# Transposing f and x from rows of four tokens, with the sigmoid and the drive term walking by row position

## The chip, the cores and the metric

The kernel runs on one core of a Trainium2 chip. The metric is the time on the device in microseconds, the median of several runs. A run of this kernel can fall into a slower state: the unchanged kernel gave 400.4 to 402 us in most of its runs and 409 to 437 us in some, on several chips. A ratio of two kernels is the mean time of one's fast runs over the mean time of the other's fast runs of the same rounds, so it is not quite the ratio of the medians that are quoted.

Names: PE is the tensor engine, PEld its weight loads, ACT the scalar engine, DVE the vector engine, POOL GpSimd, which issues the fetches of f and x, SP the engine that issues the transposing DMAs and the output stores. In a chain of waits, a q behind a name is that engine's sequencer, and "issue" is time for which the profile shows no wait.

## The reference, cut to what matters

```python
# x, f_logit: (4, 6144, 256); lower_bound: (256,)
sig = 1.0 / (1.0 + np.exp(-f_logit))
f = lower_bound + (1.0 - lower_bound) * sig
for t in range(S):                       # a recurrence over the tokens
    h = f[:, t] * h + (1.0 - f[:, t]) * x[:, t]
    y[:, t] = h
# then, for all 24576 tokens:
g = np.maximum(y @ w1, y @ w2)           # 256 -> 1024
out = g @ w_out                          # 1024 -> 256
```

## The kernel before

The work goes in 48 blocks of 512 tokens. Feature numbers lie on partitions, tokens along the free dimension. So f and x have to be transposed: the first blocks by the tensor engine, the other 44 (chunks of 1,024 tokens) by transposing DMAs from a bf16 scratch copy in DRAM. Per block there are four dependent steps: the sigmoid `u` on ACT, the decay `ff = 1 + nom*u` on DVE, the drive term `v = u*x` on DVE, and the scan over the tokens on DVE, which gives `y`. PE then multiplies: `dT` is the first layer, evicted by ACT as `rt`; `psO` is the second layer, evicted by DVE as `osb`. (max(a, b) = a + relu(b - a), so `dT` holds y(w2 - w1), ACT takes the relu, and y times w1 w_out goes straight into `psO`; the factor 1 - lower_bound of y lies in these weights.)

```python
def cross(c):                                   # one chunk: two transposing DMAs
    nt = chunks[c][2]
    for s in range(2):
        if by_xbar(c, s):
            dst = inpool.tile([P, KC, CH], BF16, name=("fT", "xT")[s])
            nc.sync.dma_start_transpose(
                out=dst[:, :, 0:nt], in_=held[c, s][0:nt, :])
            held[c, s] = dst
# ...
def gate(j):                                    # the sigmoid
    # ...
    nc.scalar.activation(
        out=like(u[:, :, 0:nb], fT), in_=fT, func=AF.Sigmoid, scale=-1.0)
# ... in scan_steps(j): decay(0), decay(1), drive, scan(0), scan(1)
def drive():
    xT = turned[j, 1]
    nc.vector.tensor_tensor(
        out=like(v[:, :, 0:nb], xT), in0=like(u[:, :, 0:nb], xT), in1=xT, op=ALU.mult)
# ... the steady loop; a turn works on block j's matmuls and prepares block j + 1
    gates = {}
    if j + 1 < NBLK and by_xbar(blocks[j + 1][3], 0):
        gates[0] = j + 1
    if j + 2 < NBLK and not by_xbar(blocks[j + 2][3], 0):
        gates[FC // 2] = j + 2
    # ...
    for fc in range(FC):
        first_layer(j, fc)                      # two matmuls to dT, ACT evicts to rt
        second_layer(j - 1, fc)                 # five matmuls to psO
        # ...
        if fc in gates:
            gate(gates[fc])
        if fc == 0 and 2 < j < NBLK - 1:
            scans = scan_steps(j + 1)
        if fc < len(scans):
            scans[fc]()
```

The sigmoid of block j + 1 is issued on ACT behind the first eviction of block j. And `dT` has three PSUM buffers.

## Time and profile before

| | before |
|---|---|
| time, median of 3 | 400.79 us (400.66 to 400.88) |
| the profiled run | 430.05 us, a slow one; span 428.3 us |
| PE, ACT, DVE busy | 392.8, 268.5, 248.7 us |
| u, v, one instruction | 1,054 and 688 ns |
| undisturbed period of a block | 7.82 us |

From the page of the kernel before: the busy times, the counts of DMA packets, the queue that holds the transposes and output stores, and the shares of the chain of waits that ended last.

```profile
PE 392.8 (92%) x2744; PEld 296.8 (69%) x2792; DVE 248.7 (58%) x359; ACT 268.5 (63%) x447; POOL 26.4 (6%) x58
...
DMA packets 103377, 77.01 MB, mean 180 GB/s; under 512 B 93552, under 2 KB 94064, under 8 KB 102640
...
q1 hardware_dynamic: 100512, 51.13, 66.7%
...
PE 46%; DMA 34%; SPq 15%; ACT 3%; DVE 1%; issue 1%; ACTq 0%
```

The chain gives 34% to DMAs, but this run is a slow one, 29 us longer than the timed ones. Durations of single instructions can be taken from it (`u` and `v` take 1,051 and 684 ns in the fast run e1, too); its waits belong to the slow state. The fast profile nearest to this kernel is that of run e1 below (wide rows, but the old compute); its chain is nearly all PE, and there too a block takes 7.82 us (`u` starts at 329.67 and 337.49):

```profile
PE 94%; DMA 2%; DVE 2%; issue 1%; SPq 1%; DVEq 0%
```

The groups of instructions of the kernel before; the columns are busy us and mean ns of one, then the engine's idle time before them and what ended most of it.

```profile
L389 ACT ACTIVATE rt<-dT 128x512 bf16<-128x512 f32 x384 | 219.2, 598 | 104.1 <-PE dT L381 100.0
L381 PE MATMUL dT<-y,wd 128*128 128x512 bf16 x720 | 219.5, 384 | 21.3 <-ACT rt L389 19.5
...
L190 ACT ACTIVATE u<-fT 128x1024 bf16<-128x1024 bf16 x44 | 46.4, 1054 | 35.5 <-DMA fT<-scr_1_91 18.2
L220 DVE TENSOR_TENSOR v<-u,xT 128x1024 bf16<-128x1024 bf16 x44 | 30.3, 688 | 3.8 <-DMA xT<-scr_0_92 1.8
```

One undisturbed block on DVE, from the timeline of the kernel before (start, duration):

```profile
375.32 0.62 DVE L209 TENSOR_SCALAR ff<-u,nom 128x512 bf16<-128x512 bf16 x2 [1.38 <-ACT u L190]
375.85 0.68 DVE L220 TENSOR_TENSOR v<-u,xT 128x1024 bf16<-128x1024 bf16 x1
377.16 0.69 DVE L430 COPY osb<-psO 128x512 f32<-128x512 f32 x1 [0.63 <-PE psO L410]
377.77 2.45 DVE L233 TENSOR_TENSOR_SCAN y<-ff,y,v 128x512 bf16<-128x512 bf16 x2
```

DVE has gaps of 1.38 and 0.63 us here: the recurrence has room inside PE's period.

### The profile page before, as it was taken

The page shows a single profiled execution, that of the slowest core. Times are in us where ns is not written, and L with a number is a line of the kernel's source. Part 1 is how long each engine was busy: PE and PEld are TensorE (multiplying, and loading weights), DVE is VectorE, ACT ScalarE, POOL GpSimd, SP SyncE. Part 2 cuts the span into 40 slices and gives each one's busy share as a digit, 9 for nine tenths or more (in the row PEclk, how much of TensorE's full clock was granted, in tenths as well). Part 3 has the DMA queues.
Part 4 walks back from the last instruction along what each step waited for, and adds up shares of the span by engine and source line. Part 5 has one row for each costly group of instructions (what it writes and reads, how often), then busy time and mean ns, then how long its engine had stood idle before and what let it go on. Part 6 is the DMA issues. An engine that isn't in the chain of part 4 may idle for free.

```text
span 428.3 us, 6970 instructions
## 1 busy us (share of the span) xinstructions
PE 392.8 (92%) x2744; PEld 296.8 (69%) x2792; DVE 248.7 (58%) x359; ACT 268.5 (63%) x447; POOL 26.4 (6%) x58
## 2 busy tenths in 40 slices
PE   3999979798789999998997899999998999999996
PEld 1677756576557777776775577767676777777775
DVE  5785637455357566564653557657547656567551
ACT  3656656557366676675673666756657676776762
POOL 1400000000000000000000000000000000000000
PEclk9999999999989999999999699999999999999999
DMA  7999999999999999999998999999999999998112
GB/s 245 222 220 198 123 157 141 137 169 252 81 240 226 119 239 233 112 248 168 183 237 75 218 158 186 250 145 170 219 131 231 226 216 164 268 157 179 79 69 100
DMA packets 103377, 77.01 MB, mean 180 GB/s; under 512 B 93552, under 2 KB 94064, under 8 KB 102640
## 3 DMA queue, kind: packets, MB, share of 16 engines
q1 hardware_dynamic: 100512, 51.13, 66.7%
q0 software_dynamic: 2544, 25.17, 36.1%
q8 instruction: 22, 0.36, 0.4%
q10 hardware_dynamic: 288, 0.26, 0.2%
q14 instruction: 11, 0.09, 0.1%
HBM read 53.48 MB, written 48.23 MB: 237 GB/s over the span
## 4 chain that ended last, share of the span: by engine, by line
PE 46%; DMA 34%; SPq 15%; ACT 3%; DVE 1%; issue 1%; ACTq 0%
PE psO L410 25%; DMA fT<-scr_0_90 20%; PE dT L381 19%; SPq L153 13%; DMA fT<-scr_1_91 12%; ACT u L190 2%; DMA w1n_110<-in_moe_w_dram 2%; SPq L433 1%; PE psO L352 1%; ACT rt L389 1%; PE tT L180 1%; PE psO L365 0%; SPq L121 0%; DVE osb L430 0%; DVE y L233 0%
## 5 line engine op out<-in xcount | busy, mean ns | idle before, releaser
L389 ACT ACTIVATE rt<-dT 128x512 bf16<-128x512 f32 x384 | 219.2, 598 | 104.1 <-PE dT L381 100.0
L381 PE MATMUL dT<-y,wd 128*128 128x512 bf16 x720 | 219.5, 384 | 21.3 <-ACT rt L389 19.5
L410 PE MATMUL psO<-wob,rt 128*128 128x256 bf16 x1536 | 230.7, 274 | 2.7 <-issue 0.4
L410 PEld LDWEIGHTS <-rt 128*128 128x128 bf16 x1536 | 170.7, 114 | 41.4 <-issue 1.1
L233 DVE TENSOR_TENSOR_SCAN y<-ff,y,v 128x512 bf16<-128x512 bf16 x88 | 107.9, 1268 | 0.1
L430 DVE COPY osb<-psO 128x512 f32<-128x512 f32 x94 | 64.7, 690 | 59.0 <-PE psO L410 58.9
L381 PEld LDWEIGHTS <-wd 128*128 128x128 bf16 x768 | 75.8, 99 | 33.2 <-issue 24.6
L209 DVE TENSOR_SCALAR ff<-u,nom 128x512 bf16<-128x512 bf16 x94 | 29.0, 351 | 105.0 <-ACT u L190 105.0
L410 PE MATMUL psO<-w_109,y 128*128 128x256 bf16 x384 | 74.0, 275 | 0.0
L410 PEld LDWEIGHTS <-y 128*128 128x128 bf16 x384 | 43.4, 113 | 42.6 <-issue 3.5
L190 ACT ACTIVATE u<-fT 128x1024 bf16<-128x1024 bf16 x44 | 46.4, 1054 | 35.5 <-DMA fT<-scr_1_91 18.2
L220 DVE TENSOR_TENSOR v<-u,xT 128x1024 bf16<-128x1024 bf16 x44 | 30.3, 688 | 3.8 <-DMA xT<-scr_0_92 1.8
L98 POOL DMA_DIRECT2D scr_0_90<-in_f_logit_dram x11 | 5.4, 493 | 149.7 <-DMA fT<-scr_0_90 149.7
L98 POOL DMA_DIRECT2D scr_1_91<-in_f_logit_dram x11 | 5.3, 486 | 148.8 <-DMA fT<-scr_1_91 148.1
L233 DVE TENSOR_TENSOR_SCAN y<-ff,v 128x512 bf16<-128x512 bf16 x6 | 7.0, 1208 | 0.0
L98 POOL DMA_DIRECT2D scr_0_92<-in_x_dram x11 | 5.4, 488 | 18.7 <-DMA xT<-scr_0_92 16.9
L98 POOL DMA_DIRECT2D scr_1_93<-in_x_dram x11 | 5.3, 486 | 15.7 <-DMA xT<-scr_1_93 14.9
L190 ACT ACTIVATE u<-tT 128x1024 bf16<-128x1024 bf16 x3 | 3.2, 1058 | 4.3 <-PE tT L180 4.3
L352 PE MATMUL psO<-ident_f,w1n_110 128*128 128x128 f32 x8 | 1.9, 422 | 3.4 <-DMA w1n_110<-in_moe_w_dram 3.4
L341 ACT ACTIVATE wd<-wdf,om 128x128 bf16<-128x128 f32 (+1 forms) x6 | 2.2, 428 | 4.3 <-DVE wdf L333 4.3
L352 PEld LDWEIGHTS psO<-ident_f,w1n_110 128*128 128x128 f32 x8 | 1.6, 221 | 3.7 <-issue 3.7
L220 DVE TENSOR_TENSOR v<-u,tT 128x1024 bf16<-128x1024 bf16 x3 | 3.6, 1216 | 0.0
(49 smaller groups left out, 45.1 us busy)
## 6 DMA issues: line engine op xcount, KB each, us to landing
out_dram<-osb SPq DMA_DIRECT2D x47, 512.0 KB, 4.8
scr_0_90<-in_f_logit_dram POOLq DMA_DIRECT2D x11, 512.0 KB, 7.5
scr_0_92<-in_x_dram POOLq DMA_DIRECT2D x11, 512.0 KB, 12.4
scr_1_91<-in_f_logit_dram POOLq DMA_DIRECT2D x11, 512.0 KB, 7.9
scr_1_93<-in_x_dram POOLq DMA_DIRECT2D x11, 512.0 KB, 13.6
fn<-in_f_logit_dram POOLq DMA_DIRECT2D x3, 256.0 KB, 7.9
xn<-in_x_dram POOLq DMA_DIRECT2D x3, 256.0 KB, 8.6
w2n_112<-in_moe_w_dram SPq DMA_DIRECT2D x1, 512.0 KB, 6.5
```

What stands on the lines that cost most here:

```text
L98: nc.gpsimd.dma_start(out=scr[0:nt, :].rearrange("(p i) d -> p (i d)", p=P), in_=src.rearrange("(p i) d -> p (i d)", p=P),)
L153: nc.sync.dma_start_transpose(out=dst[:, :, 0:nt], in_=held[c, s][0:nt, :])
L180: nc.tensor.transpose(dst, src, ident[:])
L190: nc.scalar.activation(out=like(u[:, :, 0:nb], fT), in_=fT, func=AF.Sigmoid, scale=-1.0)
L209: nc.vector.tensor_scalar(out=ff[:, h, 0:nb], in0=u[:, h, 0:nb], scalar1=nom[:, h : h + 1], scalar2=1.0, op0=ALU.mult, op1=ALU.add,)
L220: nc.vector.tensor_tensor(out=like(v[:, :, 0:nb], xT), in0=like(u[:, :, 0:nb], xT), in1=xT, op=ALU.mult,)
L233: nc.vector.tensor_tensor_scan(out=y[:, h, 0:nb], data0=ff[:, h, 0:nb], data1=v[:, h, 0:nb], initial=init, op0=ALU.mult, op1=ALU.add,)
L352: nc.tensor.transpose(pt[:, kc, q, :], half(w1n, g)[:, kc, 2 * r + q], ident_f[:])
L381: nc.tensor.matmul(dT[:, 0:nb], lhsT=wd[:, kc, fc * P : (fc + 1) * P], rhs=y[:, kc, 0:nb], start=(kc == 0), stop=(kc == KC - 1),)
L389: nc.scalar.activation(out=rt[:, 0:nb], in_=dT[:, 0:nb], func=AF.Relu)
L410: nc.tensor.matmul(ps[:, r, :], lhsT=left, rhs=right, start=(s == 0 and (r == 0 or j == NBLK - 1)), stop=(s == n - 1 and (r == 1 or j == N ...
L430: nc.vector.tensor_copy(out=osb[:, 2 * g : 2 * g + 2, :], in_=ps[:])
```

## The change

The intent is to make the source rows of the transposing DMA longer. A row of 512 B holds one token; the change reads rows of 2 KB, four tokens. The transpose then delivers tokens 0, 4, 8, ... together, then 1, 5, 9, ..., and so on. The sigmoid and the drive term therefore walk by row position: they read `fT` and `xT` contiguously, and write `u` (and read `u` and write `v`) at a stride of 4 elements, 8 B, so that `u` and `v` come out in token order.

```diff
+    RT = 4
+    wide_rows = (True, True)
@@ cross(c)
-                dst = inpool.tile([P, KC, CH], BF16, name=("fT", "xT")[s])
-                nc.sync.dma_start_transpose(
-                    out=dst[:, :, 0:nt], in_=held[c, s][0:nt, :]
-                )
-                held[c, s] = dst
+                dst = inpool.tile([P, RT, KC, CH // RT], BF16, name=("fT", "xT")[s])
+                nc.sync.dma_start_transpose(
+                    out=dst[:].rearrange("p i k r -> p (i k) r"),
+                    in_=held[c, s][0:nt, :].rearrange("(r i) d -> r (i d)", i=RT),
+                )
+                held[c, s] = dst[:].rearrange("p i k r -> p k r i")
@@ gate(j)
+        out = like(u[:, :, 0:nb], fT)
+        if by_xbar(blocks[j][3], 0):
+            out, fT = by_row(out), by_row(fT)
+        nc.scalar.activation(out=out, in_=fT, func=AF.Sigmoid, scale=-1.0)
+    def by_row(t):
+        return t if len(t.shape) == 3 else t.rearrange("p k m i -> p k i m")
@@ drive()
+            operands = [like(v[:, :, 0:nb], xT), like(u[:, :, 0:nb], xT), xT]
+            if by_xbar(c, 1):
+                operands = [by_row(t) for t in operands]
  ... (cut: like() takes m from its source; slices by o // RT; the old forms under else)
```

More of the change, by code (lines that the diff above doesn't have):

```diff
@@ L151, in cross @@
             if by_xbar(c, s):
-                dst = inpool.tile([P, KC, CH], BF16, name=("fT", "xT")[s])
-                nc.sync.dma_start_transpose(
-                    out=dst[:, :, 0:nt], in_=held[c, s][0:nt, :]
-                )
-                held[c, s] = dst
+                if wide_rows[s]:
+                    dst = inpool.tile([P, RT, KC, CH // RT], BF16, name=("fT", "xT")[s])
[4 more added lines that the diff above has]
+                    held[c, s] = dst[:].rearrange("p i k r -> p k r i")
+                else:
+                    dst = inpool.tile([P, KC, CH], BF16, name=("fT", "xT")[s])
+                    nc.sync.dma_start_transpose(
+                        out=dst[:, :, 0:nt], in_=held[c, s][0:nt, :]
+                    )
+                    held[c, s] = dst
     def turn_steps(j):
@@ L162, in turn_steps @@
             if by_xbar(c, s):
-                turned[j, s] = held[c, s][:, :, o : o + nb]
+                if wide_rows[s]:
+                    turned[j, s] = held[c, s][:, :, o // RT : (o + nb) // RT, :]
+                else:
+                    turned[j, s] = held[c, s][:, :, o : o + nb]
                 continue
@@ L189, in gate @@
         fT = turned[j, 0]
-        nc.scalar.activation(
-            out=like(u[:, :, 0:nb], fT), in_=fT, func=AF.Sigmoid, scale=-1.0
-        )
+        out = like(u[:, :, 0:nb], fT)
+        if by_xbar(blocks[j][3], 0):
+            out, fT = by_row(out), by_row(fT)
+        nc.scalar.activation(out=out, in_=fT, func=AF.Sigmoid, scale=-1.0)
         us[j] = u
@@ L197, in like @@
             return t
-        return t.rearrange("p k (m i) -> p k m i", m=P)
+        return t.rearrange("p k (m i) -> p k m i", m=src.shape[2])
+    def by_row(t):
+        return t if len(t.shape) == 3 else t.rearrange("p k m i -> p k i m")
     def scan_steps(j):
@@ L219, in drive @@
             xT = turned[j, 1]
+            operands = [like(v[:, :, 0:nb], xT), like(u[:, :, 0:nb], xT), xT]
+            if by_xbar(c, 1):
+                operands = [by_row(t) for t in operands]
             nc.vector.tensor_tensor(
-                out=like(v[:, :, 0:nb], xT),
-                in0=like(u[:, :, 0:nb], xT),
-                in1=xT,
-                op=ALU.mult,
+                out=operands[0], in0=operands[1], in1=operands[2], op=ALU.mult
             )
```

## The prediction

> **What bounds the kernel now.** The tensor engine, in the timed runs. The profiled run (430.05 us against 400.79 timed) is no fair picture of them.
>
> - In undisturbed stretches (timeline, from 347 us on) a block of 512 tokens repeats every 7.82 us: 16 matmuls of 512 columns and 40 of 256.
> - The steady loop starts at 40.0 us. Without stalls, its 45 periods would have to start at 419.97 - 45 x 7.82 = 68.1 us. So some 28 us of the profile are stalls of PE.
> - The chain of waits charges them to the transposing DMAs: 20% + 12% on fT. They land 16.1 and 15.5 us after issue (xT: 9.4 and 9.1); ACT waits 35.5 us for fT, PE 19.5 us for ACT's evictions.
> - 428.3 - 28 = 400.3 us of span, plus the 1.75 us by which this run's time exceeds its span, is 402. The timed runs took 400.79: they have practically none of these stalls. I blame the recording of 103,377 DMA packets.
>
> **What the change moves.** No instruction is added or reordered.
>
> 1. The 44 transposes move the same 512 KB, from 256 rows of 2 KB in place of 1,024 of 512 B. 93,552 packets are under 512 B, about 2,048 per transpose: 256 B each. If wide rows let a packet carry more, that count and the landing times fall.[...] I expect 256 B packets to stay, since contiguous 512 B rows are read so now. Then landing changes little, or worsens with the stride.
> 2. The drive term v (44 x 688 ns) loses step 1 on u and v.[...] The slow v from PSUM takes 1,216 ns, so I expect 1.22 us: +0.53 us per block, +23 us of DVE in all (248.7 to about 272).
> 3. The sigmoid u (1,051 ns) writes at a stride; I expect 1.05-1.15 us.
>
> **How much is critical.** Of (1), nothing in timed runs. Of (2): in the loop, v ends 0.63 us before the psO is ready that the copy after it needs, and the scans end at 380.22 us, 0.65 us before PE needs y at 380.87. The +0.53 us is absorbed before the copy; 0.1 and then 0.65 us are left.
>
> **Prediction.** 400.8 us: the same. Range 399.7 to 404.0. Faster by over 2%: 0.02 (PE has no 8 us to give). Within 2%: 0.90. Slower by over 2%: 0.08.
>
> **What the profile would show.** v<-u,xT at 1.2 us; u<-fT at 1.05; the same 7.82 us period; packets under 512 B near 93,500 if rows don't matter, far fewer if they do. The profiled span may move (405 to 440) alone.
>
> **What would make this wrong.** [...]v over 1.95 us, or u and v together over 1.28 us longer, puts the recurrence on PE's path; each further 0.1 us costs about 4.4 us over 44 blocks. Reads of 256 B at a 2 KB stride so slow that transposes miss their two-block lead: the timed runs would stall as the profile does. Or timed runs that do hide several us of DMA stalls, which shorter landings would save.

`v` at 1.22 us, an estimate from the 1,216 ns of `v` from PSUM in the profile before, is +0.53 us per block, `u` at 1.05 to 1.15 us is next to nothing, both are absorbed, and the sum is 400.8 us, the same.

## The result

| | before | after |
|---|---|---|
| time, median of 4 | 400.84 us (one of the 4 slow, 409.82) | 472.24 us (471.55 to 473.03) |
| ratio of fast runs | | 1.1784 (95%: 1.1754 to 1.1813), slower |
| u, v, one instruction | 1,054 and 688 ns | 2,512 and 2,471 ns |
| period of a block | 7.82 us | 9.44 us |

The profiled run of the changed kernel is a fast one, span 471.1 us. The same lines of its page:

```profile
PE 407.5 (87%) x2744; PEld 291.7 (62%) x2792; DVE 315.0 (67%) x359; ACT 321.3 (68%) x447; POOL 26.7 (6%) x58
...
DMA packets 103377, 77.01 MB, mean 163 GB/s; under 512 B 93552, under 2 KB 94064, under 8 KB 102640
...
q1 hardware_dynamic: 100512, 51.13, 43.8%
...
DVE 53%; ACT 25%; PE 11%; issue 7%; DMA 2%; SPq 1%; ACTq 0%
```

The number of packets is the same to the last one: with rows of 2 KB, too, the transposes go in packets of 256 B (both traces list 90,112 of exactly that size, 2,048 for each of the 44 transposes). DMAs have gone from the chain; ACT and DVE are in their place. The groups:

```profile
L406 ACT ACTIVATE rt<-dT 128x512 bf16<-128x512 f32 x384 | 216.9, 612 | 129.2 <-PE dT L398 128.3
L398 PE MATMUL dT<-y,wd 128*128 128x512 bf16 x720 | 224.7, 382 | 49.5 <-DVE y L250 44.4
...
L206 ACT ACTIVATE u<-fT 128x1024 bf16<-128x1024 bf16 x44 | 110.5, 2512 | 0.0
L240 DVE TENSOR_TENSOR v<-u,xT 128x1024 bf16<-128x1024 bf16 x44 | 108.7, 2471 | 0.0
```

`u` and `v` take 2.4 and 3.6 times as long, and PE waits 44.4 us for `y`. No engine is at its limit, though: ACT and DVE are busy 68% and 67%. The chain in order of time over one block shows why this still costs (start, duration, what):

```profile
399.32 2.53 ACT u L206
401.85 0.02 issue
401.87 0.04 DVE ff L226
401.91 0.23 issue
402.14 0.35 DVE ff L226
402.49 2.38 DVE v L240
404.87 0.52 DVE osb L447
405.39 2.37 DVE y L250 x2
407.76 0.04 issue
407.80 0.39 PE dT L398
408.19 0.02 issue
408.21 0.02 ACTq L406
408.23 0.04 issue
408.27 0.04 ACT rt L406
408.31 0.45 issue
408.77 2.50 ACT u L206
```

This is a loop through three engines: `u` of a block, its decay, its drive term, a copy that stands between, its two scans, its first matmul, the eviction of that, and only then the `u` of the next block, which is queued behind that eviction. This turn takes 408.77 - 399.32 = 9.45 us; over the whole chain, from the `u` that starts at 41.01 to the one at 446.55, 43 turns take 9.43 us each. 44 turns at 9.43 in place of 7.82 us are 71 us more, and the measured difference is 472.24 - 400.84 = 71.4 us. In that loop the slower `u` and `v` stand with +1.46 us (2,507 - 1,051 ns, the medians) and +1.78 us (2,470 - 687). Without them it would take about 6.2 us, so by this estimate the kernel before had about 1.6 us of its 7.82 per block to spare (the expectations below were written with 9.44 us and so with 1.62).

### The profile page after: what moved, and what is told of

It is laid out like the page before. It is cut to its first block, busy times and chain, and to the rows that moved or that the text cites. A ratio compares the mean times of both kernels' runs of the same rounds, so it can differ in the third digit from the quotient of the medians.

```text
span 471.1 us, 6970 instructions
## 1 busy us (share of the span) xinstructions
PE 407.5 (87%) x2744; PEld 291.7 (62%) x2792; DVE 315.0 (67%) x359; ACT 321.3 (68%) x447; POOL 26.7 (6%) x58
## 2 busy tenths in 40 slices
DMA packets 103377, 77.01 MB, mean 163 GB/s; under 512 B 93552, under 2 KB 94064, under 8 KB 102640
## 3 DMA queue, kind: packets, MB, share of 16 engines
q1 hardware_dynamic: 100512, 51.13, 43.8%
q0 software_dynamic: 2544, 25.17, 32.8%
## 4 chain that ended last, share of the span: by engine, by line
DVE 53%; ACT 25%; PE 11%; issue 7%; DMA 2%; SPq 1%; ACTq 0%
ACT u L206 24%; DVE v L240 22%; DVE y L250 22%; PE dT L398 6%; DVE osb L447 5%; PE psO L427 4%; DVE ff L226 4%; DMA w1n<-in_moe_w_dram 2%; ACT rt L406 1%; PE psO L369 1%; PE tT L193 1%; PE psO L382 0%; SPq L123 0%; ACTq L406 0%; SPq L465 0%
## 5 line engine op out<-in xcount | busy, mean ns | idle before, releaser
L398 PE MATMUL dT<-y,wd 128*128 128x512 bf16 x720 | 224.7, 382 | 49.5 <-DVE y L250 44.4
L206 ACT ACTIVATE u<-fT 128x1024 bf16<-128x1024 bf16 x44 | 110.5, 2512 | 0.0
L240 DVE TENSOR_TENSOR v<-u,xT 128x1024 bf16<-128x1024 bf16 x44 | 108.7, 2471 | 0.0
L250 DVE TENSOR_TENSOR_SCAN y<-ff,y,v 128x512 bf16<-128x512 bf16 x88 | 107.7, 1264 | 0.1
L398 PEld LDWEIGHTS <-wd 128*128 128x128 bf16 x768 | 71.8, 98 | 44.1 <-DVE y L250 22.3
L427 PE MATMUL psO<-w,y 128*128 128x256 bf16 x384 | 73.1, 272 | 0.0
L100 POOL DMA_DIRECT2D scr<-in_f_logit_dram x22 | 11.0, 498 | 315.5 <-DMA fT<-scr 314.7
L100 POOL DMA_DIRECT2D scr<-in_x_dram x22 | 10.8, 489 | 38.2 <-DMA xT<-scr 34.2
L369 PE MATMUL psO<-ident_f,w1n 128*128 128x128 f32 x16 | 3.1, 352 | 3.2 <-DMA w1n<-in_moe_w_dram 3.2
L369 PEld LDWEIGHTS psO<-ident_f,w1n 128*128 128x128 f32 x16 | 2.7, 215 | 3.7 <-issue 3.7
L350 DVE TENSOR_TENSOR wdf<-w2n,w1n 128x512 f32<-128x512 f32 (+1 forms) x5 | 4.4, 906 | 0.4 <-DMA w1n<-in_moe_w_dram 0.4
```

Source lines behind the costliest of these rows:

```text
L100: nc.gpsimd.dma_start(out=scr[0:nt, :].rearrange("(p i) d -> p (i d)", p=P), in_=src.rearrange("(p i) d -> p (i d)", p=P),)
L206: nc.scalar.activation(out=out, in_=fT, func=AF.Sigmoid, scale=-1.0)
L240: nc.vector.tensor_tensor(out=operands[0], in0=operands[1], in1=operands[2], op=ALU.mult)
L250: nc.vector.tensor_tensor_scan(out=y[:, h, 0:nb], data0=ff[:, h, 0:nb], data1=v[:, h, 0:nb], initial=init, op0=ALU.mult, op1=ALU.add,)
L350: nc.vector.tensor_tensor(out=wdf[:, :, cols].rearrange("p kc (q m) -> p kc q m", q=n), in0=half(w2n, g)[:, :, qs], in1=half(w1n, g)[:, :, ...
L369: nc.tensor.transpose(pt[:, kc, q, :], half(w1n, g)[:, kc, 2 * r + q], ident_f[:])
```

## The experiments

Theory A: the strided accesses make `u` and `v` slow, and they count as far as the serial loop has nothing to spare. Rival B: the wide-row transposes themselves disturb the kernel. Rival C: ACT and DVE have simply too much work. What makes a strided access slow, reading or writing, was open too.

### One half of the change at a time

Run e1: wide-row transposes, but the compute reads and writes as in the kernel before; the result is wrong.

```diff
-                    held[c, s] = dst[:].rearrange("p i k r -> p k r i")
+                    held[c, s] = dst[:].rearrange("p i k r -> p (i k r)").rearrange(
+                        "p (k n) -> p k n", k=KC
+                    )
-                    turned[j, s] = held[c, s][:, :, o // RT : (o + nb) // RT, :]
+                    turned[j, s] = held[c, s][:, :, o : o + nb]
```

> The wide-row transposes alone: sigmoid and drive term read and write contiguously as in the kernel before (result wrong on purpose). Theory A (the strided sigmoid and drive term lengthen the serial loop of a block): u back at 1.05 us, v at 0.69 us, time 400 to 402. Theory B (the wide-row transposes disturb the kernel, by their traffic into SBUF or by landing late): time near 472, u and v stay near 2.5 us. Landing of fT in the profile near 5 to 6 us if wide rows themselves make the transposes cheaper, near 16 us if the 5.7 us of the changed kernel came only from its slower pace.

Measured: fast runs of 400.6 to 401.84 us (a fourth run was slow, 435.05), ratio to before 1.0001. `u` 1,051 ns, `v` 684 ns; fT landed 6.2 us after its issue.

Run e2: the transposes of the kernel before, the strided compute of the changed one. Its output is wrong, which doesn't matter for the time.

```diff
-                        out=dst[:].rearrange("p i k r -> p (i k) r"),
-                        in_=held[c, s][0:nt, :].rearrange("(r i) d -> r (i d)", i=RT),
+                        out=dst[:].rearrange("p i k r -> p (i k r)").rearrange(
+                            "p (k n) -> p k n", k=KC
+                        ),
+                        in_=held[c, s][0:nt, :],
```

> The strided sigmoid and drive term alone, exactly the operands of the changed kernel, with the transposes of the kernel before (result wrong on purpose). Theory A: u 2.5 us, v 2.47 us, period 9.44 us, time 470 to 474. Theory B: near 401, u and v near 1.05 and 0.69 (or 1.2) us.

Measured: 471.55 us (471.42 to 471.72), ratio 1.1755. From the page of e2:

```profile
q1 hardware_dynamic: 100512, 51.13, 43.4%
...
L208 ACT ACTIVATE u<-fT 128x1024 bf16<-128x1024 bf16 x44 | 110.4, 2509 | 0.0
L242 DVE TENSOR_TENSOR v<-u,xT 128x1024 bf16<-128x1024 bf16 x44 | 108.7, 2470 | 0.0
```

So the strided compute alone is the whole loss, and B falls. This pair answers the intent of the change as well. At the same pace and with ample time, the queue of the transposes and stores took 43.4% of the DMA engines' time with narrow rows, and fT landed after 5.2 us; with wide rows it was 43.8% and 5.7 us. Nearer to the old pace it is no different: fT landed after 6.4 us with narrow rows (e4, below) and after 6.2 with wide ones (e1). Wide rows bought nothing that these profiles show.

### One tensor at a time

Run e3 has `wide_rows = (True, False)`, run e4 has `(False, True)`; both results are correct.

> Only f by wide rows: u is written at a stride (+1.46 us), v is contiguous (0.69 us). Theory A with one serial loop per block: in the changed kernel the loop took 9.44 us with +3.24 us in it, so it has 7.82 - (9.44 - 3.24) = 1.62 us to spare and +1.46 us is hidden: 401 to 403. If instead the costs act separately (each engine's own load), f alone gives about 1.46/3.24 of the 71 us: 432. The tighter slack of the prediction (1.28 us) would give +0.18 us per block, 408.

> Only x by wide rows: u contiguous (1.05 us), v with u and v at a stride (+1.78 us). Theory A with 1.62 us to spare: +0.16 us per block over 44 blocks, about 408. If the costs act separately: about 440. The tighter slack of the prediction (1.28 us): +0.5 us per block, about 423.

Measured for e4: 407.56 us (fast runs 407.20 to 407.88; the fourth was slow, 435.78), ratio 1.0157. The loop sum gives 44 x (1.78 - 1.62) = 7 us. Its chain names PE alone (93%), but the wait is in its timeline, hidden in the length of a pair of matmuls:

```profile
331.65 2.44 DVE L250 TENSOR_TENSOR_SCAN y<-ff,y,v 128x512 bf16<-128x512 bf16 x2
333.77 0.75 PE L398 MATMUL dT<-y,wd 128*128 128x512 bf16 x2
```

The second scan ends at 334.09, within the first pair of matmuls on that `y`, and the pair takes 0.75 us where the others take 0.59: 0.16 us, as forecast.

Measured for e3: 412.33 us (fast runs 411.66 to 412.91; the fourth was slow, 419.22), ratio 1.0263. That is a miss: the loop has room for +1.46 us, and still 11 us are lost. The chain of e3 shows another limit:

```profile
331.51 2.50 ACT u L206
334.00 0.43 ACT rt L406
334.44 0.04 issue
334.48 0.59 PE dT L398 x2
```

DVE isn't in it. While ACT works 2.5 us on `u`, it evicts nothing; PE fills the three `dT` buffers (pairs of matmuls at 331.30, 332.27 and 333.25) and waits for the first eviction after `u`: the fourth pair starts at 334.48, 0.04 us after that eviction. The next `u` starts at 339.57, so the period is 8.06 us, 0.24 more than 7.82, and 44 x 0.24 = 10.6 us. In the changed kernel this wait lies in the shadow of the longer loop.

### Taking the slow instructions out of the loop

Run e6: the changed kernel with the sigmoid issued half a block earlier (the first such block stays as it was). Run e7: the same, and the sigmoid cut into its two halves, two eviction slots apart. Both results are correct, and the accesses are as strided as in the changed kernel.

```diff
-            if j + 1 < NBLK and by_xbar(blocks[j + 1][3], 0):
+            if j + 1 < NBLK and j + 1 == 4:
                 gates[0] = j + 1
-            if j + 2 < NBLK and not by_xbar(blocks[j + 2][3], 0):
-                gates[FC // 2] = j + 2
+            if j + 2 < NBLK and j + 2 != 4:
+                gates[FC // 2] = j + 2          # e6
+                # e7: half 0 at FC // 2, half 1 at FC // 2 + 2, for blocks above 4
```

> The changed kernel, with the sigmoid of a block issued half a block earlier (as blocks turned by the tensor engine have it), so that it no longer stands between this block's first eviction and the next block's drive term. u and v stay at 2.5 and 2.47 us. Serial loop theory: the 2.5 us leave the loop, which shrinks to about 6.5 us; what is left is that a sigmoid of 2.5 us holds up the evictions of dT (three buffers), 0.24 us per block as with f alone: about 411 to 413. If instead the load of ACT and DVE binds: unchanged at 472.

> As before, and the sigmoid cut into its two halves (about 1.3 us each), two eviction slots apart. Serial loop theory with the dT buffers as the second limit: both are gone, 401 to 404 although u and v are as slow as in the changed kernel. ACT then works about 7.5 of 7.82 us per block; if that is already too tight, up to 410. If load binds: 472.

Measured: e6 414.25 us (413.55 to 415.48), ratio 1.033, a little above the forecast; `u` 2,514 and `v` 2,467 ns as before; the chain starts a `u` every 8.10 us and again runs over `u`, `rt` and PE without DVE. e7 402.65 us (402.61 to 404.75), ratio 1.005, with PE at 91% of the chain. From the timeline of e7, the two halves and the evictions between them:

```profile
334.98 1.35 ACT L216 ACTIVATE u<-fT 128x512 bf16<-128x512 bf16 x1
336.06 1.17 ACT L417 ACTIVATE rt<-dT 128x512 bf16<-128x512 f32 x2
337.12 1.37 ACT L216 ACTIVATE u<-fT 128x512 bf16<-128x512 bf16 x1
```

So C falls. In e7 ACT and DVE do all of the slow work (busy 318.9 and 323.3 us, against 321.3 and 315.0 in the changed kernel), and the time is within about half a per cent of the kernel before. Of the 71 us, 58 went with the order of one instruction and most of the rest with its length.

### What a strided access costs

Run e5, one look, result wrong on purpose (a single run, 475.24 us, its state unknown; only durations are taken from it): 11 forms of the sigmoid and 11 of the drive term take turns over the blocks. All work on 1,024 elements per partition.

> One look at durations, result wrong on purpose: 11 forms of the sigmoid and 11 of the drive term take turns over the 44 blocks, each on its own line. If strided writes are what costs: sigmoid with its output at a stride of 2, 4, 8, 32 elements near 2.5 us, with strided input and contiguous output near 1.05; drive term with only v at a stride near 2.47, with only u at a stride 0.69 to 1.22. If strided reads are what costs: the other way round. If it is the stride in bytes that counts[...], a stride of 2 elements costs less than 4 or 8, and 8 and 32 cost more[...]. With 4-byte output, contiguous 1.05; at a stride, near 1.05 if only elements under 4 bytes are slow, near 2.5 if any stride is.

Groups of e5, six for the sigmoid (fT is bf16; `wide` is an fp32 output) and two for the drive term:

```profile
L215 ACT ACTIVATE u<-fT 128x1024 bf16<-128x1024 bf16 x4 | 4.2, 1050 | 0.0
L217 ACT ACTIVATE u<-fT 128x1024 bf16<-128x1024 bf16 x4 | 5.4, 1357 | 0.0
L216 ACT ACTIVATE u<-fT 128x1024 bf16<-128x1024 bf16 x4 | 10.0, 2506 | 0.0
L218 ACT ACTIVATE u<-fT 128x1024 bf16<-128x1024 bf16 x4 | 19.1, 4771 | 0.0
L219 ACT ACTIVATE u<-fT 128x1024 bf16<-128x1024 bf16 x4 | 4.6, 1150 | 0.0
L222 ACT ACTIVATE wide<-fT 128x1024 f32<-128x1024 bf16 x4 | 4.5, 1126 | 0.0
L278 DVE TENSOR_TENSOR v<-u,xT 128x1024 bf16<-128x1024 bf16 x4 | 9.9, 2470 | 0.0
L279 DVE TENSOR_TENSOR v<-u,xT 128x1024 bf16<-128x1024 bf16 x4 | 4.9, 1218 | 0.0
```

In order: output contiguous; output at a stride of 2, of 4, of 8 elements; input at a stride of 4 with contiguous output; fp32 output at a stride of 2, which is 8 B as well; then the drive term with `v` alone and with `u` alone at a stride of 4. All of the forms, mean ns of one:

| stride | sigmoid on ACT | drive term on DVE |
|---|---|---|
| none | 1,050 | 684 |
| bf16 written at 2 elements (4 B) | 1,357 | 1,317 |
| bf16 written at 4 elements (8 B) | 2,506 | 2,470 |
| bf16 written at 8 elements (16 B) | 4,771 | 4,766 |
| bf16 written at 32 elements (64 B) | 4,694 | 4,681 |
| bf16 read at 2 elements | not tried | 1,219 |
| bf16 read at 4 elements | 1,150 | 1,218 |
| bf16 read at 8 elements | not tried | 2,024 |
| bf16 read at 128 elements (256 B) | 1,984 | 1,952 |
| fp32 written without a stride | 1,054 | not tried |
| fp32 written at 2 elements (8 B) | 1,126 | not tried |
| fp32 written at 4 elements (16 B) | 2,064 | not tried |
| input read and output written at 4 | 2,506 | 2,469 (u and v, the change) |
| both inputs read at 4 | | 1,220 |

Writing is what costs at 4 elements, and the two engines take almost the same time for it: 2,506 ns on ACT and 2,470 on DVE, against 1,150 and 1,218 for a read. From 2 to 4 elements a bf16 write gets longer by (2,506 - 1,357) / 2 = 575 ns for each further element of stride on ACT and by (2,470 - 1,317) / 2 = 577 on DVE; from 4 to 8 it is (4,771 - 2,506) / 4 = 566 and (4,766 - 2,470) / 4 = 574. From 8 to 32 elements the time hardly changes (4,694 and 4,681). That describes these forms; what in the chip makes the time grow so, and stop at 8, is not shown by any run. For 4-byte elements a stride costs less: 1,126 ns against 2,506 at 8 B, and 2,064 against 4,771 at 16 B. Reads are cheaper too: the drive term with only `u` at a stride takes 1,218 ns, which is the 1.22 us that the prediction wanted for the whole.

Reads, too, get slower as the stride grows: 2,024 ns at 8 elements on DVE, and at 128 elements 1,984 on ACT and 1,952 on DVE. Why a bf16 write costs more than an fp32 write at the same stride in bytes is not shown by these runs.

### The row length as a dial

Runs e10 and e11 are the changed kernel with `RT = 2` and `RT = 8`, both correct. Everything else stays.

> Rows of 2 tokens (1 KB), everything else as changed: u and v at a stride of 2 elements. From the probe: u 1.36, v 1.32 us, +0.94 us in the serial loop, below its 1.62 us to spare, and u short enough not to hold up evictions: 400.5 to 402.5. If the loss came from the wide rows or from leaving the contiguous order as such: well above, 430 or more.

> Rows of 8 tokens (4 KB), everything else as changed: u and v at a stride of 8 elements[...]. From the probe: u and v 4.77 us, +3.72 and +4.08 us; the loop becomes 9.44 + 2.26 + 2.30 = 14.0 us, 6.18 us over the 7.82: 400.8 + 44 x 6.18 = 673, 660 to 685. If the cost did not depend on the stride: 472.

Measured: e10 401.01 to 401.66 us in its fast runs (three of six were slow, 421 to 445), ratio 1.0012, with `u` and `v` at 1,352 ns each (from its profile, which is a slow one). e11 683.65 us (682.76 to 684.54), ratio 1.7055, `u` 4,772 and `v` 4,886 ns; in its chain `u` starts at 338.43 and 352.55, 14.1 us apart. The forecast was 673: it missed by 1.6%. Over the whole chain, from the `u` that starts at 40.25 to the one at 651.22, 43 turns take 14.21 us each, 0.21 more than forecast, which is 9 of the 11 us; `v` is 0.1 us slower than in the probe, and the copies (822 ns against 695 in the changed kernel) and the scans (1,304 against 1,264) are slower too. Why is not shown; PE's granted clock was 0.88.

### Other places for the permutation

Run e8 keeps the wide rows and moves the stride to the reads: `u` and `v` are written contiguously in token order, `fT` and `xT` read at 512 elements. Correct result.

```diff
     def by_row(t):
-        return t if len(t.shape) == 3 else t.rearrange("p k m i -> p k i m")
+        return t
```

> Wide rows, but sigmoid and drive term walk in token order: u and v are written without a stride, fT and xT are read at a stride of 512 elements. Correct result. If strided writes alone are slow: u 1.05 us, v 0.7 to 1.22 us, 400.5 to 402. If reads at such a stride are as slow: u 2.5, v 2.5, near 472 as the changed kernel.

Measured: 429.98 us (429.68 to 430.39), ratio 1.0719, between the two cases, so neither forecast: `u` 1,978 and `v` 1,953 ns. That is +0.93 and +1.27 us, 0.57 over the 1.62 to spare; the chain's period was 8.48 us, 0.66 over the 7.82.

Run e12 removes every stride: the fetch that casts f and x into the scratch tensors already places tokens r, r + 256, r + 512 and r + 768 of a chunk in row r. Correct result.

```diff
-                    out=scr[0:nt, :].rearrange("(p i) d -> p (i d)", p=P),
-                    in_=src.rearrange("(p i) d -> p (i d)", p=P),
+                    out=scr[0:nt, :].rearrange("(r i) d -> r i d", i=RT),
+                    in_=src.rearrange("(i r) d -> r i d", i=RT),
```

> Keeps 2 KB rows, without any stride in the compute: the fetch that casts f and x into the scratch tensors places tokens r, r+256, r+512, r+768 of a chunk in row r, so that each part that the transpose delivers is 256 tokens in order. u and v are written and read contiguously. Correct result. Theory: u 1.05, v 0.69 us, 400.4 to 402, if the fetches in pieces of 1 KB read and 512 B written keep up. If the smaller pieces delay the chunks (fetch landing well above the 5 to 8 us of the changed kernel): 404 to 440, with ACT waiting for fT.

Measured: 429.0 us (425.23 to 432.53, of which the last counts as slow), ratio 1.0735. `u` and `v` took 1,049 and 685 ns again, and the second case came true: ACT waited for DMAs. From the page of e12, the queue of the transposes and that of the fetches:

```profile
DMA packets 147729, 77.01 MB, mean 182 GB/s; under 512 B 93552, under 2 KB 139120, under 8 KB 147696
...
q1 hardware_dynamic: 100512, 51.13, 69.7%
q0 software_dynamic: 46896, 25.17, 48.0%
```

The fetches became 46,896 packets in place of 2,544, fT landed after 16.2 us, and ACT waited 28.2 us for it. The bytes are the same; the fetches' queue took 48.0% of the engines' time where it took 36.4% in e1. That the smaller pieces cause the loss is likely but not shown: the queue of the transposes, the landing and the wait also look like those of the kernel before in its slow state (66.7%, 16.1 and 35.5 us), so e12 may be caught in that state in all four runs. Six of the seven runs of the kernel before in the same round were fast.

### The kernel before once more

> The kernel before once more, for a profile of an undisturbed run. If 2 KB rows make the transposes cheaper for the DMA engines, their queue's share of the engines' time here is well above the 53.9% of the same schedule with wide rows (e1), and fT lands later than its 6.2 us. If rows don't matter: 53 to 55%, about 5 to 6 us (narrow rows with the slow compute had 43.4% and 5.2 us; wide rows 43.8% and 5.7 us). The prediction's claim that recording the packets slowed the profiled run would show as a profiled time near 430 again; otherwise near 401.

This run, the unchanged kernel, was meant to give an undisturbed profile and did not: 430.75 us (its state is unknown, as a single run), while seven other runs of the same kernel on that chip took 400.44 to 401.44. Its queue share was 66.9% and fT landed after 14.8 us. So there is no profile of the kernel before in the fast state; e1, the same schedule with wide rows, stands in for it. What sets the slow state off stays open.

No version beat the kernel before: e10 and e1 are level with it, and in e1 PE already makes up 94% of the chain.

## Why the prediction was wrong

- **PE bounds the timed runs before, and the DMA stalls of the profile are not in them: held.** With wide rows and the old compute (e1) the time was that of the kernel before, ratio 1.0001, and its chain was 94% PE and 2% DMAs. This holds as far as e1 can stand for the kernel before.
- **Packets stay at 256 B and landing changes little: held.** 93,552 packets under 512 B in both; 5.2 against 5.7 us at the same pace.
- **"I blame the recording of 103,377 DMA packets": not supported.** The profile of e1 recorded as many packets at 401.14 us, and so did those of e2, e3, e4, e6, e7 and e8, all in the fast state.
- **The step that failed is the size of two terms.** The prediction said "I expect 1.22 us" for `v` and "1.05-1.15 us" for `u`; they measured 2.47 and 2.51. So +0.53 us per block and next to nothing became +1.78 and +1.46. For `v` the prediction took the 1,216 ns of the `v` from PSUM as the whole price of a stride; that was an estimate. It is right for a read at 4 elements (1,218 ns in e5), and it leaves out the strided write, which in e5 takes 2,470 ns at 4 elements on DVE and 2,506 on ACT.
- **The slack was named well but measured short.** By the prediction's own rule, 1.28 us to spare, the real terms would have cost (3.24 - 1.28) x 44 = 86 us. The loop had 1.6 us: 71 us. The prediction had added gaps on DVE up; the chain of the changed kernel shows the true loop, through `u`, queued behind the eviction of the block before. It had also held both scans against PE's first matmul on `y`; in e4 that pair of matmuls had begun (333.77) before the second scan ended (334.09).
- **A limit was missing:** a sigmoid of 2.5 us holds up the evictions of three `dT` buffers, 0.24 us per block (e3).
- Its list of what would make it wrong contained what happened ("v over 1.95 us, or u and v together over 1.28 us longer"), with 0.08 given to slower. A stride that had not been measured in any trace deserved more.

## What to carry to other kernels

A strided bf16 write can cost several times a contiguous one: here 2.4 and 3.6 times at 4 elements. A read at 4 elements, or a write at 2, cost 0.1 and 0.3 us more on ACT and 0.5 and 0.6 on DVE; the loop absorbed the writes at 2 (e10). Measure a stride before trusting an estimate of its price. When an instruction gets slower, find the loop in which it stands: here +3.24 us per block cost 1.6, and issuing one instruction half a block earlier and in two pieces made nearly all of it free. Engines at two thirds of their time can still bound a kernel through the order of their queues.
